# Two blocks of w_in moved from ScalarE's load queue to SyncE's, ahead of a transposed load, and half of another block moved back

## The chip, the cores and the metric

The kernel runs on one core of a Trainium2 chip. The metric is the device time of one execution in microseconds, median of several; lower is better. The span of a profile is the time from the first to the last instruction of the program on that core; it is about 1.7 us shorter than the device time of the same execution (206.0 and 207.72 us for the first profile of before).

## The reference, cut to what matters

The reference mixes two branches over the same input x (2048 rows of 512) by a gate: attention with linear cost (A), and a gated MLP (B). The change touches only the beginning of branch B and the gate:

```python
z  = gelu(x @ w_in)              # w_in: 512 x 1376, so four blocks of 128 rows
z1, z2 = z[..., :688], layernorm(z[..., 688:])
b  = (z1 * (w_sp @ z2 + b_sp)) @ w_out
g  = sigmoid((x * gate_w).sum(-1))
out = g * a + (1 - g) * b
```

Only the right half of w_in (688 columns, for z2) is loaded at first. "Block d" below is rows 128d to 128d+127 of that half, 172 KB; each product with x takes all four blocks one after the other. "Tile t" is rows 128t to 128t+127 of x.

## The kernel before: the parts that matter

The loads at the start. SyncE and ScalarE each issue into a queue of their own; GpSimd issues one small load.

```python
nc.gpsimd.dma_start(out=gaterow[0:NDT, :], in_=gate_w.rearrange("(dt p) -> dt p", p=P))   # 1 KB
...
def load_z2w(eng, dt):
    eng.dma_start(out=w_z2[:, dt, 0:FH], in_=w_in_v[:, dt, FH:F])

nc.sync.dma_start(out=xs[:, 0, :], in_=x2[0:P, :])
nc.scalar.dma_start(out=w_z2[:, 0, 0:HF], in_=w_in_v[:, 0, FH:FH + HF])
nc.sync.dma_start(out=xs[:, 1, :], in_=x2[P:2 * P, :])
load_z2w(nc.scalar, 1)
load_z2w(nc.scalar, 2)
nc.sync.dma_start(out=w_z2[:, 0, HF:FH], in_=w_in_v[:, 0, FH + HF:F])
load_z2w(nc.scalar, 3)
...
x_dma_T(2, 2)                      # transposed load of x tiles 2 and 3, on SyncE
for h in range(2):                 # w_z1, the left half of w_in, 344 KB each
    nc.sync.dma_start(out=w_z1[:, 2 * h:2 * h + 2, :], in_=w_in_v[:, 2 * h:2 * h + 2, 0:FH])
...                                # and on SyncE, without a pause, every later load up to 61 us
```

What TensorE does meanwhile. Tiles 0 and 1 are loaded as they are and transposed on TensorE; `one(t, d, j)` multiplies tile t's block d with half j of its columns. The gate's weights go through TensorE too (`gate_T`), and become column 345 of the second halves.

```python
warm_up(6)                         # products of ones: they keep TensorE busy while it waits
warm_up(2, P)
x_T(0, ...)                        # transposes of tile 0
warm_up(3, P)
one(0, 0, 0)
x_T(1, ...)                        # transposes of tile 1
one(0, 1, 0)
warm_up(1, P)
one(1, 0, 0)
one(1, 1, 0)
gate_T()                           # waits for gaterow
one(0, 2, 0)                       # the first product with block 2
one(1, 2, 0)
for dt in range(1, 3):
    one(0, dt, 1)
    one(1, dt, 1)
for tt in range(2):                # block 3, and the second half of block 0
    one(tt, 3, 0); one(tt, 0, 1); one(tt, 3, 1)
    z2_out(tt, zps[tt])
```

Then come tile 2, tile 3, and so on, in fixed order.

The softmax here doesn't subtract the row's maximum and nothing guards it: scores larger than these inputs give would overflow.

Of the kernel before, what the change touches and what calls it, by code (L numbers as in the profile page):

```python
# [19 lines left out]
F = 1376  # L20
FH = 688
HF = FH // 2
# [13 lines left out]
def kernel(  # L36
# [14 lines left out]
    nc = tc.nc  # L51
# [12 lines left out]
    w_z2 = early.tile([P, NDT, WP], BF16, name="w_z2")  # L64
# [31 lines left out]
    w_in_v = B_w_in.rearrange("(dt p) f -> p dt f", p=P)  # L96
# [7 lines left out]
        out=ramp[:, 0, :], data0=ones32[:, :], data1=zeros[:, :], initial=0.0,  # L104
# [4 lines left out]
    for q in range(4):  # L109
        qs = slice(32 * q, 32 * q + 32)  # L110
        nc.vector.tensor_tensor(
            out=ident[qs, qs], in0=ramp[qs, 0, :], in1=ramp[qs, 1, :], op=ALU.is_equal)
# [3 lines left out]
    def load_z2w(eng, dt):  # L116
        eng.dma_start(out=w_z2[:, dt, 0:FH], in_=w_in_v[:, dt, FH:F])  # L117
# [2 lines left out]
    nc.scalar.dma_start(out=w_z2[:, 0, 0:HF], in_=w_in_v[:, 0, FH:FH + HF])  # L120
    nc.sync.dma_start(out=xs[:, 1, :], in_=x2[P:2 * P, :])
    load_z2w(nc.scalar, 1)
    load_z2w(nc.scalar, 2)
    nc.sync.dma_start(out=w_z2[:, 0, HF:FH], in_=w_in_v[:, 0, FH + HF:F])
    load_z2w(nc.scalar, 3)

    def x_dma_T(i, n=1):
        nc.sync.dma_start_transpose(out=xT[:, :, i * P:(i + n) * P], in_=x2[i * P:(i + n) * P, :])
# [2 lines left out]
    for h in range(2):  # L131
        nc.sync.dma_start(
            out=w_z1[:, 2 * h:2 * h + 2, :], in_=w_in_v[:, 2 * h:2 * h + 2, 0:FH])
    for i in range(4, 8):
        x_dma_T(i)
    for q in range(2, NCH):
        nc.sync.dma_start_transpose(
            out=xT[:, :, q * CH:(q + 1) * CH], in_=x2[q * CH:(q + 1) * CH, :]
        )
    nc.sync.dma_start(out=brow[0:NT, :], in_=B_b_sp.rearrange("(t p) -> t p", p=P))  # L140
    for qk in (1, 0):
        nc.sync.dma_start_transpose(
            out=wqkT[:, qk * NDT:(qk + 1) * NDT, :], in_=A_wqkv[:, qk * D:(qk + 1) * D])
# [4 lines left out]
    for h in range(2):  # L148
        nc.sync.dma_start(
            out=wv_sb[:, 2 * h:2 * h + 2, :],  # L150
            in_=A_wqkv[h * 2 * P:(h + 1) * 2 * P, 2 * D:3 * D].rearrange("(dt p) n -> p dt n", p=P),
        )
    for q in range(NCH):
        nc.sync.dma_start_transpose(
            out=wspT[:, :, q * CH:(q + 1) * CH], in_=B_w_sp[q * CH:(q + 1) * CH, :]
# [4 lines left out]
        out=mask4[:], in_=mask4[:], pattern=[[-32, NG]],  # L160
# [3 lines left out]
        out=mask4[:], in_=mask4[:], pattern=[[32, NG]],  # L164
# [3 lines left out]
        out=mask64[:, :, :], in_=mask4[:, :, None].to_broadcast([P, NG, DH]))  # L168
# [429 lines left out]
```

## Time and profile before

| | before |
|---|---|
| median of the first 3 runs | 207.43 us (207.28 to 207.88) |
| span of the profile | 206.0 us |
| TensorE busy | 201.2 us, 98% |

From the page of the kernel before: the busy times of the engines, and the shares of the chain that ended last (the work followed back from the last instruction to what released each step).

```profile
PE 201.2 (98%) x1518; PEld 120.4 (58%) x1536; DVE 128.7 (62%) x276; ACT 76.5 (37%) x123; POOL 45.4 (22%) x73
...
PE 95%; DMA 2%; issue 1%; ACTq 0%; DVE 0%
```

The kernel is a string of matmuls. The 2% of DMA is all at the start. The chain of waits of before in its first 16 us (start, duration, what):

```profile
1.25 0.47 ACTq L117
1.72 0.03 issue
1.75 4.61 DMA w_z<-in_B_w_in_dram
6.36 0.04 issue
6.40 9.72 PE zp L188 x65
```

The load with 4.61 us to landing is block 2, third in ScalarE's queue. It lands at 6.36 us; at 6.40 TensorE takes it up and does not stop. The list of TensorE's waits, before (total, times, longest) has only this one for data, and it is short, since TensorE had other work until 6.2:

```profile
PE zp L219 <- PEq L582: 0.8, 1, 0.8
PE zp L188 <- DMA w_z<-in_B_w_in_dram: 0.2, 1, 0.2
```

That work, from the timeline of before (start, duration, what; idle time before it and its cause would stand in brackets):

```profile
5.43 0.78 PE L188 MATMUL zp<-w_z,xT 128*128 128x344 bf16 x2
6.00 0.21 PE L282 MATMUL pq<-ident,gaterow 128*128 128x4 bf16 x1
```

The gate's transpose at 6.00 follows the products without idle time. The gate's load had landed at 5.73.

SyncE's issues in the timeline of before (start, duration, what):

```profile
1.74 0.42 SPq L124 DMA_DIRECT2D w_z<-in_B_w_in_dram  x1
2.21 1.45 SPq L128 DMA_TRANSPOSE xT<-in_A_x_dram  x1
3.71 1.08 SPq L132 DMA_DIRECT2D w_z<-in_B_w_in_dram  x2
4.83 5.28 SPq L128 DMA_TRANSPOSE xT<-in_A_x_dram  x4
10.16 4.59 SPq L137 DMA_TRANSPOSE xT<-in_A_x_dram  x2
14.87 0.51 SPq L140 DMA_DIRECT2D brow<-in_B_b_sp_dram  x1
```

A plain load occupies its issuer for 0.4 to 0.6 us, a transposed one for 1.3 and more.

### The profile page before, as it was taken

The numbers are of one execution on the slowest core, as the hardware profiler recorded it, in microseconds if no ns is written. First come the engines' busy times: TensorE is split into PE (matmuls) and PEld (weight loads), VectorE is DVE, ScalarE is ACT, GpSimd is POOL, SyncE is SP. The second block draws the span as 40 slices with busy tenths as digits, with TensorE's granted clock in tenths as the row PEclk, the third lists the DMA queues.
The fourth block names the chain that finished last, engine by engine and source line by source line (L and its number), as shares of the span: only waits on it lengthen the run. The fifth ranks groups of instructions, "written<-read, shape, count | busy, mean of one in ns | idle before, by whom it ended". The sixth has DMA issues, their size and how long they took to land.

```text
span 206.0 us, 3927 instructions
## 1 busy us (share of the span) xinstructions
PE 201.2 (98%) x1518; PEld 120.4 (58%) x1536; DVE 128.7 (62%) x276; ACT 76.5 (37%) x123; POOL 45.4 (22%) x73
## 2 busy tenths in 40 slices
PE   8999999999999999999999999999999999999994
PEld 4566666665666555556565666555455555665642
DVE  3367665746977687979797788555466553633330
ACT  2756677786222233332424042222261126001322
POOL 5020202020532426334242422222204220200000
PEclk9999999999999999999999999999999999999999
DMA  6999499999996026940412228863554767353642
GB/s 169 278 193 181 83 263 210 261 190 267 191 290 138 3 38 146 313 91 14 85 37 55 51 38 118 149 113 71 106 151 89 80 110 184 58 104 71 129 90 78
DMA packets 90099, 27.22 MB, mean 132 GB/s; under 512 B 84224, under 2 KB 90080, under 8 KB 90080
## 3 DMA queue, kind: packets, MB, share of 16 engines
q1 hardware_dynamic: 87168, 24.28, 60.9%
q10 hardware_dynamic: 2880, 2.68, 4.2%
q8 instruction: 12, 0.20, 0.4%
q14 instruction: 7, 0.06, 0.1%
q0 software_dynamic: 32, 0.00, 0.0%
HBM read 4.15 MB, written 2.10 MB: 30 GB/s over the span
## 4 chain that ended last, share of the span: by engine, by line
PE 95%; DMA 2%; issue 1%; ACTq 0%; DVE 0%
PE mm L442 36%; PE zp L188 18%; PE mm L347 13%; PE mm L481 8%; PE mm L387 7%; PE mm L479 7%; DMA w_z<-in_B_w_in_dram 2%; PE at L455 2%; PE kvacc L403 2%; PE mm L484 1%; PE zp L299 0%; ACTq L117 0%; ACTq L120 0%; PE pq L299 0%; DVE ob L491 0%
## 5 line engine op out<-in xcount | busy, mean ns | idle before, releaser
L442 PE MATMUL mm<-z2all,wspT 128*128 128x344 bf16 x512 | 79.9, 309 | 0.0
L442 PEld LDWEIGHTS <-wspT 128*128 128x128 bf16 x512 | 49.0, 98 | 25.7 <-issue 0.4
L188 PE MATMUL zp<-w_z,xT 128*128 128x344 bf16 (+1 forms) x256 | 39.1, 312 | 0.2 <-DMA w_z<-in_B_w_in_dram 0.2
L351 ACT ACTIVATE eq<-mm 128x512 bf16<-128x512 f32 x32 | 17.4, 594 | 51.3 <-PE mm L347 21.3
L188 PEld LDWEIGHTS <-xT 128*128 128x128 bf16 x256 | 24.9, 99 | 12.5 <-issue 0.3
L355 DVE TENSOR_REDUCE zs<-eq 128x64 f32<-128x1024 bf16 x16 | 19.5, 1220 | 20.3 <-ACT eq L351 20.3
L447 DVE SCALAR_TENSOR_TENSOR ucat<-mm,bT,z1all 128x344 bf16<-128x344 f32 x32 | 17.4, 544 | 21.9 <-PE mm L442 21.9
L364 POOL TENSOR_TENSOR eq<-eq,ratio 128x512 bf16<-128x512 bf16 x16 | 16.9, 1059 | 49.9 <-DVE ratio L363 41.7
L351 ACT ACTIVATE ek<-mm 128x512 bf16<-128x512 f32 x32 | 17.3, 600 | 27.1 <-PE mm L347 27.1
L495 ACT ACTIVATE ob<-mm,g_inv 128x512 bf16<-128x512 f32 (+1 forms) x16 | 10.9, 681 | 32.8 <-PE mm L484 28.3
L355 DVE TENSOR_REDUCE zs<-ek 128x64 f32<-128x1024 bf16 x16 | 19.3, 1210 | 2.8 <-ACT ek L351 2.8
L481 PE MATMUL mm<-wspT,uT 128*128 128x512 bf16 (+2 forms) x85 | 20.1, 366 | 0.0
L347 PEld LDWEIGHTS <-xT 128*128 128x128 bf16 x128 | 12.2, 98 | 12.9 <-PE mm L484 0.8
L364 POOL TENSOR_TENSOR ek<-ek,ratio 128x512 bf16<-128x512 bf16 x16 | 16.9, 1059 | 2.1 <-DVE ratio L363 1.1
L347 PE MATMUL mm<-wq_p,xT 128*128 128x512 bf16 x55 | 16.0, 379 | 0.5
L387 PE MATMUL mm<-wv_sb,xT 128*128 128x512 bf16 x64 | 16.4, 379 | 0.0
L347 PE MATMUL mm<-wk_p,xT 128*128 128x512 bf16 x61 | 16.1, 379 | 0.2
L479 PE MATMUL mm<-wspT,oT 128*128 128x512 bf16 (+2 forms) x62 | 15.6, 365 | 0.3
L206 DVE BATCH_NORM_STATS2 bn<-z2all 128x6 f32<-128x344 bf16 x32 | 14.9, 503 | 0.0
L203 ACT ACTIVATE z2all<-zp 128x688 bf16<-128x688 f32 x16 | 11.8, 744 | 6.4 <-PE zp L188 6.4
L252 ACT ACTIVATE z1all<-zp 128x688 bf16<-128x688 f32 x16 | 11.9, 744 | 5.1 <-PE zp L188 4.6
L481 PEld LDWEIGHTS <-uT 128*128 128x128 bf16 x85 | 8.1, 98 | 9.2
(72 smaller groups left out, 142.8 us busy)
## 6 DMA issues: line engine op xcount, KB each, us to landing
out_dram<-ob ACTq DMA_DIRECT2D x15, 128.0 KB, 1.7
wspT<-in_B_w_out_dram SPq DMA_DIRECT2D x2, 640.0 KB, 5.0
w_z<-in_B_w_in_dram SPq DMA_DIRECT2D x2, 344.0 KB, 5.1
w_z<-in_B_w_in_dram ACTq DMA_DIRECT2D x3, 172.0 KB, 4.6
wv_sb<-in_A_wqkv_dram SPq DMA_DIRECT2D x2, 256.0 KB, 3.1
wspT<-in_A_wo_dram SPq DMA_DIRECT2D x2, 256.0 KB, 4.0
xs<-in_A_x_dram SPq DMA_DIRECT2D x2, 128.0 KB, 2.6
uT<-ucat SPq DMA_TRANSPOSE x16, 2.8
```

Source lines behind the costliest of these rows:

```text
L188: nc.tensor.matmul(zp[:, j, 0:n], lhsT=xT[:, dt, tt * P:(tt + 1) * P], rhs=wt[:, dt, j * HF:j * HF + n], start=(dt == first), stop=(dt == ...
L206: nc.vector.bn_stats(out=bn6[:, tt, j, :], in_=z2v[:, j, :])
L252: nc.scalar.activation(out=z1all[:, tt, :].rearrange("p (j n) -> p j n", j=2), in_=zp[:, :, 0:HF], func=AF.Gelu_apprx_tanh,)
L347: nc.tensor.matmul(ps[:, :], lhsT=xT[:, dt, tt * P:(tt + 1) * P], rhs=w[:, dt, :], start=(dt == 0), stop=(dt == NDT - 1))
L351: nc.scalar.activation(out=e[:, :, a, :], in_=ps[:, :].rearrange("p (h f) -> p h f", f=DH), func=AF.Exp, scale=1.0 - 2.0 * a)
L355: nc.vector.tensor_reduce(out=z[:].rearrange("p h a -> p (h a)"), in_=e[:].rearrange("p h a f -> p (h a) f"), axis=AX.X, op=ALU.add,)
L364: nc.gpsimd.tensor_tensor(out=e[:, :, 1, :], in0=e[:, :, 1, :], in1=ratio[:, :, None].to_broadcast([P, H, DH]), op=ALU.mult)
L387: nc.tensor.matmul(v_ps[:, :], lhsT=xT[:, dt, tt * P:(tt + 1) * P], rhs=wv_sb[:, dt, :], start=(dt == 0), stop=(dt == NDT - 1))
L442: nc.tensor.matmul(gp[:, 0:HF], lhsT=wspT[:, st, tt * P:(tt + 1) * P], rhs=z2all[:, st, j * HF:(j + 1) * HF], start=(st == 0), stop=(st == ...
L447: nc.vector.scalar_tensor_tensor(out=ucat[tt % NU][:, c0 + j * HF:c0 + (j + 1) * HF], in0=gp[:, 0:HF], scalar=bT[:, tt:tt + 1], in1=z1all[ ...
L479: nc.tensor.matmul(acc, lhsT=oT[:, g, :], rhs=wo_t[:, g, c0:c1], start=(g == 0), stop=False)
L481: nc.tensor.matmul(acc, lhsT=uT[:, i + ft, :], rhs=w_main[i][:, ft, c0:c1], start=False, stop=False)
```

## The change

Its intent: block 2 is what TensorE waits for, and it is third on ScalarE. Queue blocks 2 and 3 on SyncE ahead of the transposed load, and let ScalarE take the half of block 0, which is needed later.

```diff
     nc.sync.dma_start(out=xs[:, 1, :], in_=x2[P:2 * P, :])
     load_z2w(nc.scalar, 1)
-    load_z2w(nc.scalar, 2)
-    nc.sync.dma_start(out=w_z2[:, 0, HF:FH], in_=w_in_v[:, 0, FH + HF:F])
-    load_z2w(nc.scalar, 3)
+    load_z2w(nc.sync, 2)
+    nc.scalar.dma_start(out=w_z2[:, 0, HF:FH], in_=w_in_v[:, 0, FH + HF:F])
+    load_z2w(nc.sync, 3)
```

## The prediction

> **What bounds the kernel now.** TensorE. The page has its matmuls busy for 201.2 of 206.0 us (98%), and the chain of waits is 95% TensorE, 2% DMA. That DMA piece is one wait: from 1.75 to 6.36 us the chain is block 2 of w_in (third on ScalarE, 4.61 us to landing); from 6.40 on it is matmuls with hardly a break. The list of waits gives TensorE one idle of 0.2 us for that block and none for another load of this stage.
>
> **What the change does.** It computes nothing differently; 344 KB of loads move from ScalarE's queue to SyncE's, 86 KB the other way. By the timeline a plain load occupies its issuer for 0.41 to 0.47 us.
> - SyncE issues one plain load more ahead of the transposed load of x tiles 2 and 3: at about 2.7 us instead of 2.21. It issues without a gap until 61 us, so everything behind goes out 0.47 us later.
> - ScalarE issues one less and starts its table load 0.47 us sooner; nothing waits for that.
> - Before, block 2 shared the engines with the half of block 0 and then with the transposed load's packets. Now it follows x tile 1 directly on SyncE. The Trainium skill (DMA: Bandwidth & Descriptors, "Issuing engines are not separate DMA queues") says that all issuers share 16 DMA engines and only issue time is saved; what moves here is the order inside the queues. Estimates from the packets of before (about 230 GB/s between 3.5 and 5 us): block 2 lands at 5.2 to 5.6 us, the half of block 0 at 5.2 (5.96 before, needed at 7.4), block 3 at 5.8 to 6.1 (6.89, needed at 7.3), tiles 2 and 3 at 7.0 to 7.7 (7.71).
>
> **How much is on the critical path.** Only the start of block 2's matmuls. Just before them stands the gate's transpose, which waits for its own small GpSimd load (landed 5.73) and runs at 6.00. So block 2 cannot start much before 6.15 however early it lands: a gain of about 0.2 us (0.1%). Slack elsewhere: tiles 2 and 3 are needed at about 8.0 us (12 matmuls of 0.146 us after block 2); w_z1 landed at 8.7 and 9.6, needed after 10.4; tile 4 at 10.2, needed at 15; w_phi at 25.3, needed at 27.0; the w_sp slabs have 10 us.
>
> **Predicted time:** 207.2 us, from 207.43; 8 in 10 for 206.7 to 207.9 (the three runs of before spread over 0.6 us, more than the effect). Faster by over 2%: 0.005; within 2%: 0.98; slower by over 2%: 0.015.
>
> **What would show the steps right.** Block 2 lands before 5.7 us; TensorE's 0.2 us for w_in is gone from the list of waits, and the chain begins with another load; block 2's first matmul starts at 6.1 to 6.2; SyncE's issues from the transposed load to 61 us come 0.4 to 0.5 us later; no new wait for x tiles 2 and 3; span about 0.2 us shorter.
>
> **What would make it wrong.** The transposed load, with 344 KB queued ahead of it instead of 86 KB, lands after 8.0 us: TensorE waits, and the gain becomes a loss of some tenths. The gate's small load moves with the crowding of the engines (earlier: a gain up to 0.5 us; later: none). A longer early TensorE gap delays the full clock (matmuls of 491 ns before 5.4 us, 309 after), which would cost more than either.

## The result, and the profile after

| first comparison | before | after |
|---|---|---|
| median of 4 runs | 207.36 us (207.22 to 207.88) | 207.56 us (207.46 to 207.70) |
| span of the profile | 206.0 us | 205.7 us |
| ratio after / before | | 1.0006, 95% interval 0.9987 to 1.0024 |

A ratio here is the mean time of one kernel's runs over that of the other's of the same rounds, so it is not quite the ratio of the medians. The sign is not clear: the medians say 0.2 us slower, the profiled execution was 0.3 us shorter.

From the page after, the same two lines:

```profile
PE 200.5 (97%) x1518; PEld 119.7 (58%) x1536; DVE 128.6 (62%) x276; ACT 76.5 (37%) x123; POOL 45.3 (22%) x73
...
PE 95%; DMA 2%; issue 1%; SPq 0%; DVE 0%
```

The chain of waits after, first 16 us:

```profile
1.28 0.41 SPq L121
1.69 0.05 issue
1.74 4.43 DMA w_z<-in_B_w_in_dram
6.17 0.04 issue
6.21 9.80 PE zp L188 x66
```

Block 2 still heads the chain, now issued by SyncE at 1.74. It landed at 6.17, only 0.19 us sooner, and TensorE still waits for it and, in this profile, for the gate's load too:

```profile
PE zp L188 <- DMA w_z<-in_B_w_in_dram: 0.3, 1, 0.3
PE pq L282 <- DMA gaterow<-in_gate_w_dram: 0.3, 1, 0.3
```

The same stretch of TensorE's timeline as above. Here the full clock came at 3.81 us, and it is the gate's load that the transpose waits for:

```profile
5.02 0.47 PE L188 MATMUL zp<-w_z,xT 128*128 128x344 bf16 x2
5.76 0.18 PE L282 MATMUL pq<-ident,gaterow 128*128 128x4 bf16 x1 [0.27 <-DMA gaterow<-in_gate_w_dram]
```

SyncE's issues after:

```profile
1.74 0.90 SPq L117 DMA_DIRECT2D w_z<-in_B_w_in_dram  x2
2.68 1.32 SPq L128 DMA_TRANSPOSE xT<-in_A_x_dram  x1
4.06 1.08 SPq L132 DMA_DIRECT2D w_z<-in_B_w_in_dram  x2
5.18 5.28 SPq L128 DMA_TRANSPOSE xT<-in_A_x_dram  x4
10.50 4.22 SPq L137 DMA_TRANSPOSE xT<-in_A_x_dram  x2
14.84 0.51 SPq L140 DMA_DIRECT2D brow<-in_B_b_sp_dram  x1
```

The transposed load goes out 0.47 us later, as it must with one issue more ahead of it. But the delay shrinks to 0.34 us at 10.5 and is gone at 14.84: the two transposed loads before that took 4.22 us to issue instead of 4.59. (That time varies between executions: 4.13 us in the second profile of before.)

### The profile page after: what moved, and what is told of

The parts are those of the page before. It is cut to its first block, busy times and chain, and to the rows that moved or that the text cites. A ratio compares the mean times of both kernels' runs of the same rounds, so it can differ in the third digit from the quotient of the medians. Undisturbed runs are those within 1.5% of the kernel's fastest.

```text
span 205.7 us, 3927 instructions
## 1 busy us (share of the span) xinstructions
PE 200.5 (97%) x1518; PEld 119.7 (58%) x1536; DVE 128.6 (62%) x276; ACT 76.5 (37%) x123; POOL 45.3 (22%) x73
## 4 chain that ended last, share of the span: by engine, by line
PE 95%; DMA 2%; issue 1%; SPq 0%; DVE 0%
PE mm L442 36%; PE zp L188 18%; PE mm L347 13%; PE mm L481 8%; PE mm L387 7%; PE mm L479 7%; DMA w_z<-in_B_w_in_dram 2%; PE at L455 2%; PE kvacc L403 2%; PE mm L484 1%; PE zp L299 0%; SPq L121 0%; SPq L119 0%; PE pq L299 0%; DVE ob L491 0%
## 5 line engine op out<-in xcount | busy, mean ns | idle before, releaser
L188 PE MATMUL zp<-w_z,xT 128*128 128x344 bf16 (+1 forms) x256 | 38.4, 309 | 0.3 <-DMA w_z<-in_B_w_in_dram 0.3
```

Source lines behind the costliest of these rows:

```text
L188: nc.tensor.matmul(zp[:, j, 0:n], lhsT=xT[:, dt, tt * P:(tt + 1) * P], rhs=wt[:, dt, j * HF:j * HF + n], start=(dt == first), stop=(dt == ...
```

## The experiments

All runs gave correct results. Every timed run counted as fast; before_2, only_swap and swap23 are single runs, whose state is unknown, and are used for their profiles only. The theory to be tested, A: nothing but the start of block 2's first product matters; everything after it is back to back, so the span is a constant plus that start. Its rival: something later takes shifts up or adds to them. And a second question, since block 2 landed at 6.17 and not at the predicted 5.2 to 5.6: what sets its landing?

First, what fourteen profiles show together (us; the two kernels themselves in bold; where the gate's load is on ScalarE the profile does not tell its landing; the last column is taken from the unrounded times):

| profile | gate landed | block 2 landed | start of its first product | span | span less start |
|---|---|---|---|---|---|
| **before** | 5.73 | 6.36 | 6.40 | 206.0 | 199.58 |
| **before**, second | 6.25 | 6.88 | 6.92 | 206.5 | 199.55 |
| **after** | 5.71 | 6.17 | 6.21 | 205.7 | 199.53 |
| **after**, second | 4.77 | 5.10 | 5.32 | 205.0 | 199.67 |
| **after**, third | 4.95 | 5.48 | 5.74 | 205.4 | 199.66 |
| half of the change | 5.54 | 6.97 | 7.01 | 206.6 | 199.55 |
| half of the change, second | 6.01 | 6.58 | 6.62 | 206.2 | 199.55 |
| blocks 3 and 2 swapped | 5.66 | 6.72 | 6.76 | 206.3 | 199.54 |
| blocks 1 and 2 swapped (the figures of block 1) | 5.19 | 5.55 | 5.88 | 205.6 | 199.70 |
| gate's load on ScalarE | not told | 5.36 | 6.06 | 205.9 | 199.83 |
| fill, gate's load on ScalarE | not told | 5.81 | 6.11 | 205.4 | 199.29 |
| fill, loads as changed | 5.38 | 5.86 | 6.21 | 205.5 | 199.26 |
| tiles 2 and 3 late | 6.07 | 6.54 | 6.58 | 207.7 | 201.09 |
| block 2 late | 6.03 | 9.69 | 9.74 | 211.0 | 201.23 |

The last column is the finding: 199.5 to 199.8 us wherever the order of the products is unchanged and no second wait was made. What varies between executions of one kernel is the start. (In the run with the gate's load on ScalarE the first products of block 2 still ran at half clock, which accounts for the high 199.83.)

The small spread has a pattern. Where TensorE waited for block 2 the constant is 199.53 to 199.58; where it came to the block without waiting (after's second and third profile, blocks 1 and 2 swapped) it is 199.66 to 199.70. There the third product, the first one on a second half and so in need of the gate's column, started 0.05 us after VectorE had written that column (written at 5.70, started at 5.75 in after's second profile), 0.15 us later than back to back. So once block 2 is early enough, the gate's column takes over, and about 0.15 us of an earlier start is lost again.

### The changed kernel twice more (after_again, after_3)

No edit; timed in 5 rounds each.

> The changed kernel once more, unchanged, to see whether 0.2 us can be resolved and which landing times repeat. Theory A (the gain is only the earlier start of block 2's matmuls, 0.19 us in the two profiles): ratio to before 0.998 to 1.000. Rival (it costs something elsewhere, as the medians of the first four runs, 207.56 against 207.36, would have it): ratio 1.0005 to 1.002. In the profile, block 2's landing repeats within 0.3 us of 6.17 if the queue order sets it; if it is chance it moves by more.

> The changed kernel a third time, for a third set of times and a third profile. The two kernels' starts of block 2 overlap so far (6.40 and 6.92 us before, 6.21 and 5.32 after), and so do the spans (205.1 to 206.3 in 22 runs of before, 205.0 to 205.9 in 6 of after). If the change gains a tenth or two of a microsecond on average, the ratio is 0.9985 to 1.000; if nothing, 0.9995 to 1.0005. Span less start of block 2: 199.4 to 199.8. Block 2 lands somewhere from 5.1 to 7.0.

Measured: after_again 207.37 us (206.74 to 207.65, 6 runs), ratio 0.9992 (0.9973 to 1.0011). after_3 207.06 us (206.73 to 207.60, 6 runs), ratio 0.9989 (0.9973 to 1.0005). The chain of waits of after_again has no load in it at all:

```profile
4.39 0.23 PE tp L272 x2
4.62 0.02 issue
4.64 0.30 DVE xT L278
4.94 0.04 issue
4.99 0.47 PE zp L188 x2
5.45 0.01 PE pq L282
5.46 10.68 PE zp L188 x72
```

Here block 2 landed at 5.10 and the gate at 4.77, and TensorE came to block 2 by its own pace. So the same kernel has block 2 at 6.17, 5.10 and 5.48: its landing is not a property of the kernel that one profile could give. Nor is the sign of the first comparison: three comparisons gave 1.0006, 0.9992 and 0.9989. Pooling their runs (16 of after, mean 207.32 us; the 26 of before that were timed beside them, 207.46 us; standard deviations 0.32 and 0.31) gives 0.15 us faster with a standard error of 0.10, so an approximate 95% interval from 0.35 faster to 0.05 slower. That agrees with the predicted 0.2 us and does not exclude that nothing was gained.

### The kernel before once more (before_2)

> The kernel before once more, for a second profile. In the five profiles so far, span less start of block 2's first matmul is 199.5 to 199.8 us; it should be so again. If the queue order sets block 2's landing, it lands here at 6.0 to 6.8 us (6.36 in the first profile, against 6.17 and 5.10 after the change); if single slow packets set it by chance, it may lie anywhere from 5.1 to 6.5, and the two kernels overlap.

Measured: span 206.5 us, one run of 208.18 us. Its chain:

```profile
1.74 5.14 DMA w_z<-in_B_w_in_dram
6.88 0.04 issue
6.92 9.22 PE zp L188 x62
```

The landing, 6.88, missed both expectations on the late side, 6.0 to 6.8 by a little and 5.1 to 6.5 by more; the constant held. Both profiles of before are later than all three of after. Two against three do not prove a shift, but it points the same way as the pooled times.

### Block 2 last (late2)

```diff
-    load_z2w(nc.sync, 2)
 ...
     for h in range(2):
         nc.sync.dma_start(out=w_z1[:, 2 * h:2 * h + 2, :], ...)
+    load_z2w(nc.sync, 2)
```

> Block 2 is queued behind both w_z1 loads, so that it lands at about 9.6 us instead of 6.17. Theory A (TensorE does nothing but wait for block 2 here, and all that follows is back to back): its wait for w_in grows to about 3.6 us and the time grows by as much, about 3.4 us (ratio 1.016). Rival B (the stages after it have slack that takes such a shift up, so that an early load is worth little either way): less than half of it, under 1.7 us.

Measured: 213.54 us (212.68 to 214.12, 4 runs), ratio 1.0301 (1.0274 to 1.0327): 6.0 us, where theory A expected 3.4 and the rival less than half of that. The wait itself was as expected:

```profile
PE zp L188 <- DMA w_z<-in_B_w_in_dram: 3.5, 1, 3.5
```

The rest is TensorE's clock. The granted clock is the share of full speed at which TensorE was allowed to run. Busy times of late2 in three stretches, of the products with w_in alone (stretch, length, TensorE busy and number of products, VectorE, which has none here, granted clock, DMA share, GB/s):

```profile
9.74:10.10 0.36, 0.36 (x3) 0.00 (x0) 1.00 1.37 224
10.10:13.40 3.30, 3.30 (x14) 0.00 (x0) 0.51 0.84 186
13.40:16.70 3.30, 3.30 (x24) 0.00 (x0) 0.97 1.04 220
```

From 10.1 to 13.4 us the granted clock is 0.51 and 14 products overlap the stretch, against 24 in the next one of the same length. The Trainium skill (TensorE: Matmul & The Clock Gate, "Part 1: The HAM clock gate") says that TensorE falls to half clock after an idle window of about 3.4 us and needs a busy window to come back; the trace agrees: 3.5 us of waiting, then 3.4 us of half clock (its clock record: 10.18 to 13.59). Half clock for 3.4 us costs 1.7 us, which is how 199.6 becomes 201.2. In the other three runs the mean granted clock was 0.984 and not 0.992: 1.6% of some 212 us is 3.4 us lost, as from two such windows. So theory A stands on the wait (one for one), and the rival falls (nothing later absorbs any of it); but the clock cost up to as much again as the wait, which neither theory had.

### Tiles 2 and 3 late (t23_late)

The transposed load goes behind both w_z1 loads on SyncE: the line `x_dma_T(2, 2)` moves below that loop.

> The transposed load of x tiles 2 and 3 goes behind both w_z1 loads. Two questions. Does it slow the blocks ahead of it? If so, block 3 lands by 5.9 us and block 2 by 5.3; if single slow packets alone do it, block 2 stays between 5.1 and 6.2. And what does a shorter wait cost? Tiles 2 and 3 land at about 9.0, needed at 7.1 to 8.0: TensorE waits 1 to 1.9 us, too short to cost the clock, so the time grows by that and no more, ratio 1.005 to 1.009, where the 3.5 us wait of the run with block 2 late cost 6 us.

Measured: 208.93 us (208.56 to 209.38, 4 runs), ratio 1.0072 (1.0051 to 1.0093). TensorE's waits:

```profile
PE zp L188 <- DMA xT<-in_A_x_dram: 1.4, 1, 1.4
...
PE pq L282 <- DMA gaterow<-in_gate_w_dram: 0.3, 1, 0.3
PE zp L188 <- DMA w_z<-in_B_w_in_dram: 0.3, 1, 0.3
```

A wait of 1.4 us cost 1.5 us and left the clock alone (products of 309 ns before it and after it), so the extra price of late2 comes with its longer wait of 3.5 us; no run tried a length between the two. On the second question: with no transposed load behind them the blocks were not faster, 6.54 for block 2 and 7.04 for block 3. The transposed load is not what makes them late. What does is seen in the trace's semaphore updates. A load counts to 16, one from each DMA engine, and is complete when the last has come (so says the skill, DMA: Bandwidth & Descriptors, "Why a DMA increments its semaphore by 16 and not by 1"; the trace shows sixteen updates for each of these loads). In t23_late they came thus:

```
load               12th of 16 updates   last four
gate (GpSimd)      4.88                 5.90 to 6.07
block 2 (SyncE)    5.16                 6.25 to 6.54
half of block 0    5.38                 6.52 to 6.76
block 3 (SyncE)    6.00                 6.81 to 7.04
```

Four engines are a microsecond behind the twelve others, on three queues at once, as the prediction's premise that all issuers share the engines would have it. In the packet records of that profile five packets read between 3.5 and 4.0 us took 5.8 us together, where most packets of that size (1376 bytes) took 59 ns; the four longest, started between 3.72 and 4.08, took 1.3 to 1.7 us each. The records do not name the engine, so that these packets lie on those four engines is inferred. It would also explain why the gate's 1 KB was late in most profiles: it waited for the same slow engines.

### What makes single packets slow: the gate's load, or the block itself? (gate_act, swap23, block2_second)

Three edits, each against the changed kernel:

```diff
# gate_act
-    nc.gpsimd.dma_start(out=gaterow[0:NDT, :], ...)
     load_z2w(nc.scalar, 1)
+    nc.scalar.dma_start(out=gaterow[0:NDT, :], ...)
# swap23
-    load_z2w(nc.sync, 2)
+    load_z2w(nc.sync, 3)
     nc.scalar.dma_start(out=w_z2[:, 0, HF:FH], ...)
-    load_z2w(nc.sync, 3)
+    load_z2w(nc.sync, 2)
# block2_second
-    load_z2w(nc.scalar, 1)
-    load_z2w(nc.sync, 2)
+    load_z2w(nc.scalar, 2)
+    load_z2w(nc.sync, 1)
 ...
-            z_one(zps[tt], tt, w_z2, FH + 1, dt, j, first=j)
+            z_one(zps[tt], tt, w_z2, FH + 1, (0, 2, 1, 3)[dt], j, first=2 * j)
```

> The gate's 1 KB load leaves GpSimd's queue and goes third on ScalarE. Theory S (the GpSimd load, whose packets lie between 3.7 and 5.4 us, is what slows single packets to 200 to 900 ns at that time): the slow packets are gone, block 2 lands at about 5.3 us, and TensorE starts it before 5.7 us, 0.5 us sooner. Rival M (block 2's own rows are slow to read) or P (whatever is read then is slow): slow packets stay, block 2 lands at 6.0 to 6.4, the gate lands earlier than 5.2, TensorE's wait for the gate goes and its wait for block 2 grows from 0.3 to about 0.8 us, and the time does not move.

> Blocks 3 and 2 change places on SyncE's queue; the matmuls still take block 2 first. Theory P (time or place sets the slow packets): block 3 now lands at 6.0 to 6.3 with packets of 200 ns and more from 3.4 to 5.0 us, block 2 at about 6.7, and TensorE starts 0.5 us later. Theory M (block 2's own rows are slow to read): block 3 lands before 5.7, and the slow packets begin later, at about 4.2 us.

> Blocks 1 and 2 change places, in the loads and in the order of the first two tiles' products, so that TensorE has the same work in the same order of landing. In seven profiles the load third on SyncE met single packets of 200 to 1200 ns from 3.5 to 4.5 us, whether it was block 2 or 3. Theory P (the time or the place in the queue sets them): block 1, now third on SyncE, meets them in the same stretch and lands at 5.1 to 7.0. Theory R (the first reads of the later rows of w_in, blocks 2 and 3, are slow): the slow packets are block 2's and lie at 2.8 to 3.4 us on ScalarE's queue, block 1 lands at 5.0 to 5.4 without them. Time: within 0.002 of before in either case.

Measured, packets above 300 bytes that took over 150 ns, by the half microsecond in which they started (number / us together):

```
               3.0-3.5   3.5-4.0   4.0-4.5   4.5-5.0
before         1/0.2     2/0.5     12/4.5    4/0.8
before_2       0/0.0     5/2.7     4/1.0     8/4.3
after          1/0.5     9/3.8     7/3.1     4/1.0
after_again    0/0.0     6/1.6     6/1.4     2/0.6
after_3        1/0.2     7/1.7     2/0.5     0/0.0
gate_act       0/0.0     7/3.2     4/1.1     0/0.0
swap23         0/0.0     9/4.5     1/0.3     1/0.4
block2_second  1/0.2     6/3.0     4/1.1     2/0.6
```

- gate_act (207.46 us, ratio 0.9996, 0.9975 to 1.0018): the slow packets stay without any GpSimd load, so the small load is not their cause. The gate's load shows five semaphore updates, the last at 4.37 us, earlier than 5.2 as the rivals expected, if that is its landing. Block 2 landed at 5.36, earlier than they expected, and within what chance gives. TensorE waited for neither; it came to block 2 at 6.06 by its own pace, because in this execution the full clock came only at about 6.6 us. And the edit had a price of its own, in SyncE's list of waits:

```profile
SPq L128 <- DMA w_z<-in_B_w_in_dram: 0.9, 1, 0.9
```

The transposed load's issue now waits until the first half of block 0 has landed (it goes out at 3.50 us instead of 2.68): one load more on these two queues, and it comes to use the semaphore that the first one still holds.

- swap23 (one run, 208.02 us): block 3, now in block 2's place, met the slow packets in the same stretch and landed at 5.95, near the expected 6.0 to 6.3; block 2 landed at 6.72, and TensorE started at 6.76. The block's own rows are not the cause.
- block2_second (207.30 us, ratio 1.0002, 0.9983 to 1.0021): block 1 met them in the same stretch. Theory P (the time or the place) is left, R falls.

So what is read from 3.5 to 5 us has a few packets of 0.15 to 1.7 us (the longest in t23_late and only_swap_2), whatever block it is, with or without the GpSimd load. Why is open; no run here separates the time from the place in the queue, or looks into the memory.

### Half of the change (only_swap, only_swap_2)

Block 2 and the half of block 0 change queues; block 3 stays on ScalarE. So block 2 stands directly ahead of the transposed load:

```diff
-    load_z2w(nc.scalar, 2)
-    nc.sync.dma_start(out=w_z2[:, 0, HF:FH], ...)
+    load_z2w(nc.sync, 2)
+    nc.scalar.dma_start(out=w_z2[:, 0, HF:FH], ...)
     load_z2w(nc.scalar, 3)
```

> Half of the change: block 2 third on SyncE and the half of block 0 third on ScalarE, but block 3 stays last on ScalarE. If the change works through block 2's place alone, block 2 lands at 5.1 to 6.2 us as after the change. Block 3, on the queue that the transposed load does not share, should no longer have all 16 of its increments bunched behind the stall of that load, as in the three profiles with block 3 ahead of it on SyncE.

> Half of the change once more, now timed. In its one profile the transposed load stood directly behind block 2 on SyncE; that load's first packets all ended together at 6.9 us, and the last four increments of block 2 came only then (6.94 to 6.97), while the full change, with block 3 between, had block 2 at 5.1 to 6.2. Theory H (the transposed load holds the increments of the load just ahead of it): block 2's last increments come again at or after the common end of those first packets, and the half change is no faster than before, ratio 0.9995 to 1.003. Rival (chance, one slow profile): block 2 lands apart from that end, at 5.1 to 6.2, and the ratio is 0.998 to 0.9995 like the full change's.

Measured: only_swap, one run of 208.26 us, block 2 at 6.97; its expectation missed twice, since block 3's updates were bunched as well (6.98 to 7.19), though it sat on the other queue. only_swap_2: 207.66 us (207.20 to 208.16, 6 runs), ratio 1.0009 (0.9988 to 1.0030). Its chain:

```profile
1.74 4.85 DMA w_z<-in_B_w_in_dram
6.58 0.04 issue
6.62 9.51 PE zp L188 x64
```

The packet records show one more thing here, and in every other profile: the first 256-byte packets of the transposed load end together, however early each began. In only_swap_2, 18 of them started between 5.18 and 6.14 us and all ended between 6.43 and 6.46; in the first profile of after, 19 between 5.29 and 6.36, ending at 6.53 to 6.57. In both half-changes block 2's last updates came just after that common end (6.94 to 6.97 after 6.9; 6.49 and 6.58 after 6.46). Theory H is therefore not refuted, and the time fell in the range it gave. But it is not shown either: an engine that is late with block 2 is also late at the transposed load, and would produce the same order. At 1.0009 with an interval of 0.2% either way, half the change cannot be told from before nor from the whole.

### A trial at something faster (fill, fill_gp)

If the span is a constant plus the start, one can shrink the constant: multiply block 1's second halves, which have long landed, before block 2 instead of after it.

```diff
         gate_T()
-        one(0, 2, 0)
-        one(1, 2, 0)
-        for dt in range(1, 3):
-            one(0, dt, 1)
-            one(1, dt, 1)
+        one(0, 1, 1)
+        one(1, 1, 1)
+        for j in range(2):
+            one(0, 2, j)
+            one(1, 2, j)
```

That is fill_gp. fill has the gate's load on ScalarE as in gate_act as well, `gate_T` directly after `one(0, 1, 0)`, and one warm-up product less.

> A trial at something faster than both: the changed kernel with the gate's load third on ScalarE, the gate's transpose moved ahead, and block 1's second halves multiplied before block 2 instead of after it, so that 2 matmuls (0.3 us) fill the wait. If span is a constant plus the start of block 2's matmuls, the constant falls by about 0.3 us to 199.3; ratio 0.997 to 0.9995. If the clock or the landings dominate, 0.999 to 1.001.

> The last trial: the changed kernel with only the order of the products altered (block 1's second halves directly after the gate's transpose, ahead of block 2); every load stays where the change put it, since in the former trial the gate's load on ScalarE held the transposed load's issue back to 3.4 us from 2.7. Span less start of block 2's first product should be 199.3 instead of 199.6; block 2 is taken at the latest of its landing and 0.3 us after the gate's transpose. Where block 2 binds (as in the first profile) 0.3 us is won, where the gate or TensorE's own pace binds, nothing: ratio to before 0.998 to 1.000, to be told from the changed kernel's 0.9993 only if all of it comes.

Measured: fill 207.49 us (207.11 to 208.29, 6 runs), ratio 1.0009 (0.9989 to 1.0030); fill_gp 207.45 us (207.18 to 207.70, 6 runs), ratio 0.9998 (0.9981 to 1.0015). The constant fell to 199.3 in both profiles, as expected, and the time did not follow. For fill_gp the profile shows why; TensorE's waits:

```profile
PE zp L188 <- DVE w_z L283: 0.3, 1, 0.3
```

Block 1's second halves need the gate's column, and that goes from TensorE through VectorE back to memory: transpose at 5.46, next product at 5.92. Formerly block 2's first two products covered this, all but 0.15 us of it where TensorE did not wait for block 2. So the hole was filled from one end and reopened at the other: block 2 had landed at 5.86, and its first product started at 6.21. For fill, whose profile has no such wait, the slower runs (up to 206.5 us of span) were not profiled; why they were slow is open. Neither beats the changed kernel.

## Why the prediction was right, and where it was not

- **The time.** Predicted 207.2 us, about 0.2 us gained, "same"; measured "same", pooled gain 0.15 us with a standard error of 0.10. "Same" within 2% is a weak test of an effect of 0.1%, and even the sign of the gain is not established; the first comparison alone had it the other way. The mechanism, that only the start of block 2's products counts and the rest follows one for one, is shown by span less start (199.53 to 199.83 over ten profiles with the products' order unchanged and no added wait) and by t23_late and late2.
- **Off the critical path.** Right: no new wait for tiles 2 and 3 (7.76, 6.98 and 7.03 us in the three profiles of after), for w_z1 or for w_phi.
- **"Block 2 lands at 5.2 to 5.6 us".** Wrong as a statement about the kernel: 6.17, 5.10 and 5.48, of which only the last lies in the range. The failed step took the mean rate of the packets as the time of a load. A load is complete with the last of its sixteen updates, and in t23_late the last four came about a microsecond after the twelfth; that single slow packets (up to 1.7 us) make these late is inferred. Likewise the half of block 0 came at 6.53, 5.76 and 5.67 (5.2 predicted), and block 3 at 6.75, 5.95 and 6.02 (5.8 to 6.1).
- **"Block 2 cannot start much before 6.15".** The 6.15 was read from one execution, and its reason was misread. In that profile the gate's transpose at 6.00 waited for TensorE's half clock (the trace's clock record has the full clock from 6.57 us on, and two products took 0.78 us where they take 0.47 at full clock), not for the gate's load (landed at 5.73): it stands at 6.00 in only_swap and 5.99 in gate_act as well, where the full clock was as late. The gate's load sets it only where it lands later than TensorE's pace, as in the first profile of after (5.71, transpose at 5.76) and in before_2 (6.25, 6.30). Both move: the load landed between 4.77 and 6.25 us, and the full clock came anywhere from 3.5 to 6.8 us. So the after kernel started block 2 at 5.32 and 5.74 as well. That its first profile started block 2 at 6.21, close to the predicted 6.1 to 6.2, was luck: the block itself, landed at 6.17, held it there, and not the gate. Of the signs named, "TensorE's 0.2 us for w_in is gone" failed in the first profile (0.3 us) and held in the two others, and so did "Block 2 lands before 5.7 us".
- **"SyncE's issues ... come 0.4 to 0.5 us later" until 61 us.** Wrong: 0.47 at the transposed load, 0.34 at 10.5 us, none at 14.84. The transposed loads issued there took 4.22 us instead of 4.59 (but 4.13 in before_2); that they are held back by how fast the engines take them is likely, but no run tested it. It cost nothing, since nothing waited there.
- **The clock.** Not in the prediction's sums: it took TensorE's pace at the start as fixed, where the arrival of the full clock moves it. And late2 shows what a long gap costs: 3.5 us of waiting cost 6.0 us.

## What to carry to other kernels

Find the one moment from which the critical engine no longer stops, and check on several profiles that the span less that moment is constant; then a change ahead of it is worth what it moves that moment (here to within 0.3 us, unless the clock falls back), and a change elsewhere nothing as long as it makes no new wait. A landing time read from one profile is a sample: here it spread by a microsecond within one kernel, five times the effect in question, so look at several profiles of each before you argue from tenths of a microsecond, and note that 42 timed runs still left 0.2 us of uncertainty. A long wait of TensorE can cost more than itself through the clock: here 6.0 us for a wait of 3.5, but 1.5 us for one of 1.4.

## What the Trainium skill lacked or had wrong

- TensorE: Matmul & The Clock Gate, "Part 1: The HAM clock gate", says that the first change to full clock varies by ±500 ns. In the profiles here, all with TensorE busy from 0.85 us on, the trace's clock record has the full clock from 3.47 us at the earliest (after_again) and from 6.79 at the latest (only_swap), a spread of 3.3 us; thirteen have such a record, and where TensorE was at work the durations of its products agree. That is about one whole window of the free-running kind that the same section describes, and the section's ±500 ns does not fit.
- DMA: Bandwidth & Descriptors has no figure for how much the landing of one load varies between executions of one kernel: block 2, 172 KB, landed 3.4 to 4.4 us after its issue in three profiles of the changed kernel, through single 1376-byte packets of up to 0.7 us beside a usual 59 ns (in t23_late five packets took 5.8 us together).
- No page says that the first packets of a transposed load end together. In all fourteen profiles 13 to 24 of them, those that took over 0.15 us, did so, within 0.1 us in most and at most 0.4 us, after waits of up to 1.5 us.
- DMA: Bandwidth & Descriptors, "Issuing engines are not separate DMA queues", calls the issue time that is saved usually small beside the load. For the plain loads here that fits (0.4 to 0.6 us), for transposed ones less: one tile held SyncE for 1.3 us, and the four transposed loads of w_sp held it for 36 us (25.13 to 61.35). The section also leaves out a price of another kind: in gate_act a load of 1 KB added to ScalarE's queue delayed the issue of another load on SyncE by 0.8 us (3.50 instead of 2.68), through a semaphore that an earlier load still held.
